# First two FFN steps in halves, free banks for six chunks' products, a new order of the work

## The chip, the cores and the metric

The kernel runs on one core of one Trainium2 chip. The metric is the device time of one execution, in microseconds: the median over runs, of which three were made of the kernel before.

## What is computed

A linear attention with decay, and a feed-forward block (FFN) on its output. Cut to what matters:

```python
for t in range(S):                      # attention, B=4, H=8, S=768, D=48
    cur = u * kt outer vt
    y[t] = rt @ (state + cur)
    state = w * state + kt outer vt     # w per head and channel, constant over t
x = y.transpose(0, 2, 1, 3).reshape(3072, 384)
h = x @ w_in                            # 384 -> 2048
sp = maximum(h, 0) + log1p(exp(-abs(h)))
out = (h * erf(sp)) @ w_out             # 2048 -> 384
```

## The kernel before, in words

**Attention.** The sequence is cut into pieces of 128 tokens. With four batches this makes 24 chunks of 128 tokens; chunk g is piece g // 4 of batch g % 4. For a chunk, VectorE or GpSimd scale k and r by powers of the decay (L220, L224), TensorE forms the 128x128 products A of eight heads (L307) in two PSUM banks, and VectorE copies their upper triangle (`copy_predicated`, L313 for chunks 0 to 7, L319 and L322 after that) over a tile `am` that holds the diagonal (made by ScalarE at L288 or by VectorE or GpSimd at L290). Then TensorE forms the chunk's output y from `am` and, from chunk 4 on, from the carried state `sbd` (L339), and the state's increment ds (L358). The diagonal's factors come from L270, L273, L277, and for the first four chunks from L233 and small products (L239, L248). y is split into a high part (ScalarE, L379) and the remainder (VectorE, L382) of the tile x: four chunks fill one x tile of 512 tokens.

**FFN.** The matrices are multiplied in fp32r, which keeps fewer bits, so every operand is split into a high and a low part and three products are summed. A step n of the FFN is one block of 512 tokens times one of 16 slices of 128 hidden columns: there are 96 steps. `f1` (L398 to L407) makes h with 9 matmuls of 128x512; ScalarE and VectorE make the activation (L412 to L437: a, b, z, c, d, e, g), its high part gh (L443, ScalarE) and low part gl (L448, VectorE or GpSimd); `f2` (L453 to L465) adds 9 matmuls to three accumulator banks. The weights arrive as 64-bit floats, are turned to fp32 by bit operations (L125 to L135) and split (L137), 16 pieces in all. Blocks 0 and 1 are done in two halves of the hidden columns, with their partial sums stored to DRAM and loaded again.

**What sets the order.** Every engine runs its instructions in the order in which the program issues them, and that order is written out by hand in one long string, `ORDER` (L694 to L757). Each word is one step: a letter for the operation, a number for the chunk or FFN step, then `+` for GpSimd, `*` for ScalarE, nothing for the default engine, and after `@` the PSUM banks. The words that this document speaks of:

- L load of a chunk (SyncE's queue), F load of a weight piece, C its conversion, W some dummy matmuls;
- K and R scaling of k and r (L220, L224), E their product (L233), B, J, H, Qc the small products that give the first chunks' diagonal (L239, L245, L248, L253), Qa, Qb, Qc for later chunks the same by L270, L273, L277, M the diagonal tile (L288, L290), N a scaled k (L228, or ScalarE's copy L266), V transposes (L259);
- A, P, Y, D: products A (L307), triangle copies P (L313), output y (L339), state increment ds (L358); S the state's update (L370, L372, L376);
- Xa, Xb: x high (L379) and x low (L382);
- f, a, b, z, c, d, e, g, h, l, p: FFN step (f L405, z L421, g L437, h L443, l L448, p L464);
- O the outputs and partial sums, Z the check at the end (L510 to L514).

PSUM has eight banks: three with the tag `h` (the h of FFN steps and others), two `A0`, `A1`, three accumulators `acc0` to `acc2`. A step whose bank or input isn't ready waits, and everything behind it on its engine with it.

**The end.** After the last step the kernel counts decay values outside a range (L510 to L513), every engine loads the count to a register (`values_load`, L514, which shows as `TENSOR_LOAD`), and a branch (L596) runs a second, general version of the whole computation if the count isn't zero. It is zero here, so that version is jumped over.

```python
    with tc.If(rv > 0, preferred_fallthrough_block=False), ...
```

Of the kernel before, what the change touches and what calls it, by code (L numbers as in the profile page):

```python
# [697 lines left out]
Q4a+ Q4b V2 L5a W3 M20* L3b C10b Q4c T0 D3@0 C10c P20 Y2 M40+ M41* C10d L5b Q5a C10e C10f+ K5+ N4 F01 R5+ Q5b Q5c X1b
A4@h1 N2* S3a* S3b* Y3@h X2a D2@0 X3a X2b S2b* X3b f0 C01a P41 S2a C01b P40 L6a C01c R6 M51* L6b Q6a+ M50* a0 K6 C01d
b0 F02 z0 Y4@h X4a A5 P51 C01e C01f+ f1 D4 c0 P50 d0 Q6b+ X4b S4b S4a e0 g0 L7a C02a C02b Q6c C02c a1 b1 Y5 X5a X5b z1  # L700
f2 M60* c1 C02d C02e K7 M61+ A6 d1 N5 f3 P61 D5 P60 C02f+ S5b h0 a2 N6+ e1 S5a g1 F11 L7b C11a b2 C11b h1 l0 Y6 z2 a3
b3 D6 X6a S6b S6a c2 d2 l1+ e2 f4 C11c p0 p1 a4 Q7a C11d z3 C11e g2 h2 C11f Q7b+ Q7c f5 l2+ c3 X6b F03 C03a C03b C03c
# [124 lines left out]
```

## Time and profile before

| | |
|---|---|
| median of 3 runs (510.79, 512.91, 512.54) | 512.54 us |
| profiled execution, its own time | 510.69 us |
| span of that execution, first to last instruction | 508.9 us |
| TensorE busy | 493.1 us, 97% |
| ScalarE busy | 403.3 us, 79% |
| VectorE busy | 338.1 us, 66% |
| GpSimd busy | 183.1 us, 36% |
| DMA, mean rate over the span | 93 GB/s |
| granted TensorE clock, mean | 0.996 |

The profiled execution was 1.85 us shorter than the median. Busy shares are averages over the whole span: the page's second part cuts it into 40 slices, and the first three slices and the last one differ from the rest.

### The profile page before, as it was taken

To read this page: it belongs to the slowest core of one execution; us is meant where nothing else is said; L and a number is where in the kernel's file an instruction comes from. 1 tells how busy PE (TensorE), PEld (TensorE's weight loads), DVE (VectorE), ACT (ScalarE), POOL (GpSimd) and SP (SyncE) were. 2 spreads that over 40 slices of the span, in tenths; PEclk is the share of its full clock that TensorE was granted. 3 is DMA by queue.
4 is the path that set the end of the run, shared out by engine and by line. 5 is a ranking of instruction groups with operands and counts; after the bars stand their busy time and mean duration, and the time that the engine had idled before them with its cause. 6 is when DMAs were issued, how large, how long until landed. Compare 5 with 4: busy or idle time off the path is not lost.

```text
span 508.9 us, 10505 instructions
## 1 busy us (share of the span) xinstructions
PE 493.1 (97%) x4176; PEld 389.5 (77%) x4176; DVE 338.1 (66%) x610; ACT 403.3 (79%) x747; POOL 183.1 (36%) x167
## 2 busy tenths in 40 slices
PE   7789999999999999999999999999999999999994
PEld 3567777877877777787878888787888888878883
DVE  7999999898876956765868644646556453353442
ACT  4788999999997666778776777878778777987982
POOL 6657335433265544625354033513312221202110
PEclk9999999999999999999999999999999999999998
DMA  8656343613605151250131350020120000000001
GB/s 309 222 215 247 123 154 125 216 62 116 243 23 182 64 166 50 90 190 13 51 134 43 105 190 0 7 87 1 63 91 0 1 2 0 33 31 1 0 1 68
DMA packets 14007, 47.34 MB, mean 93 GB/s; under 512 B 1664, under 2 KB 2560, under 8 KB 13952
## 3 DMA queue, kind: packets, MB, share of 16 engines
q1 hardware_dynamic: 13952, 46.61, 26.7%
q8 instruction: 35, 0.57, 0.5%
q14 instruction: 20, 0.16, 0.1%
HBM read 40.31 MB, written 6.29 MB: 92 GB/s over the span
## 4 chain that ended last, share of the span: by engine, by line
PE 86%; DVE 8%; ACT 2%; DMA 1%; issue 1%; POOL 1%; DVEq 0%; ACTq 0%; POOLq 0%
PE h L405 38%; PE acc L464 36%; PE y L339 6%; PE A L307 3%; PE ds L358 1%; DVE s L421 1%; DVE am L313 1%; DMA out_dram<-o 1%; DVE att L220 1%; DMA o<-part 1%; DVE wt L129 1%; DVE gl L448 1%; ACT gh L443 0%; DVE att L224 0%; DVE s L437 0%
## 5 line engine op out<-in xcount | busy, mean ns | idle before, releaser
L405 PE MATMUL h<-x,wih 128*128 128x512 f32 x576 | 183.1, 399 | 1.4 <-DVE s L437 1.0
L448 POOL TENSOR_TENSOR gl<-s,gh 128x512 fp32r<-128x512 f32 x52 | 69.0, 1328 | 213.9 <-ACT gh L443 186.6
L405 PEld LDWEIGHTS h<-x,wih 128*128 128x128 f32 x576 | 106.7, 188 | 28.3 <-DVE s L437 1.9
L464 PE MATMUL acc<-gh,woh 128*128 128x512 f32 x288 | 115.0, 399 | 0.0
L464 PE MATMUL acc<-gl,woh 128*128 128x512 f32 x288 | 114.1, 396 | 0.2 <-DVE gl L448 0.2
L405 PE MATMUL h<-x,wil 128*128 128x512 f32 x288 | 113.7, 395 | 0.0
L464 PE MATMUL acc<-gh,wol 128*128 128x512 f32 x288 | 113.7, 395 | 0.0
L437 DVE SCALAR_TENSOR_TENSOR s<-s,h 128x512 f32<-128x512 f32 x96 | 65.6, 685 | 61.4 <-ACT s L433 61.1
L421 DVE SCALAR_TENSOR_TENSOR s<-s,h 128x512 f32<-128x512 f32 x96 | 65.7, 686 | 59.3 <-ACT s L416 42.4
L425 ACT ACTIVATE s<-s 128x512 f32<-128x512 f32 x96 | 60.2, 628 | 37.3 <-DVE s L421 37.3
L443 ACT CAST gh<-s 128x512 fp32r<-128x512 f32 x96 | 58.7, 614 | 21.6 <-DVE s L437 16.0
L412 ACT ACTIVATE s<-h 128x512 f32<-128x512 f32 x96 | 56.7, 592 | 15.6 <-PE h L405 15.1
L464 PEld LDWEIGHTS acc<-gl,woh 128*128 128x128 f32 x288 | 54.2, 188 | 14.0 <-DVE gl L448 1.5
L464 PEld LDWEIGHTS acc<-gh,woh 128*128 128x128 f32 x288 | 54.1, 188 | 13.4 <-ACT gh L443 0.2
L405 PEld LDWEIGHTS h<-x,wil 128*128 128x128 f32 x288 | 54.1, 188 | 12.9
L464 PEld LDWEIGHTS acc<-gh,wol 128*128 128x128 f32 x288 | 54.2, 188 | 12.7
L416 ACT ACTIVATE s<-s 128x512 f32<-128x512 f32 x96 | 60.4, 632 | 2.1
L433 ACT ACTIVATE s<-s 128x512 f32<-128x512 f32 x96 | 60.3, 629 | 2.1
L429 ACT ACTIVATE s<-s 128x512 f32<-128x512 f32 x96 | 60.4, 629 | 1.9
L448 DVE TENSOR_TENSOR gl<-s,gh 128x512 fp32r<-128x512 f32 x44 | 31.6, 719 | 13.7 <-ACT gh L443 13.1
L290 POOL TENSOR_TENSOR am<-ident,q 128x512 f32<-128x512 f32 x17 | 19.0, 1118 | 25.9 <-DVE q L277 17.6
L339 PE MATMUL y<-am,att 128*32 128x128 f32 x768 | 25.5, 273 | 1.5 <-DVE am L313 1.3
(98 smaller groups left out, 514.0 us busy)
## 6 DMA issues: line engine op xcount, KB each, us to landing
att<-in_att_dram SPq DMA_DIRECT2D x24, 512.0 KB, 4.0
att<-in_att_dram SPq DMA_DIRECT2D x20, 608.0 KB, 5.6
raw<-in_win_dram SPq DMA_DIRECT2D x8, 768.0 KB, 6.4
raw<-in_wout_dram SPq DMA_DIRECT2D x8, 768.0 KB, 4.7
out_dram<-o SPq DMA_DIRECT2D x17, 256.0 KB, 2.2
part<-o SPq DMA_DIRECT2D x6, 256.0 KB, 3.8
o<-part SPq DMA_DIRECT2D x6, 256.0 KB, 4.2
att<-in_early_dram SPq DMA_DIRECT2D x4, 224.0 KB, 8.2
```

The source lines that it names most:

```text
L339: nc.tensor.matmul(out=y[r:r + 32, q, :], lhsT=lhsT, rhs=rhs, start=r not in new, stop=True, skip_group_check=True)
L405: nc.tensor.matmul(out=h, lhsT=w[:, f, q, :], rhs=x[:, xi, q, :], start=k == 0, stop=k == 8)
L412: nc.scalar.activation(out=s1, in_=e["h"], func=AF.Tanh, bias=FB0, scale=FA0)
L416: nc.scalar.activation(out=s1, in_=s1, func=AF.Tanh, bias=FB1, scale=FA1)
L421: nc.vector.scalar_tensor_tensor(out=e["s"], in0=e["s1"], scalar=FG, in1=e["h"], op0=ALU.mult, op1=ALU.add)
L425: nc.scalar.activation(out=s, in_=s, func=AF.Tanh, bias=FB2, scale=FA2)
L429: nc.scalar.activation(out=s, in_=s, func=AF.Square, bias=FB3, scale=FA3)
L433: nc.scalar.activation(out=s, in_=s, func=AF.Square, bias=FB4, scale=FA4)
L437: nc.vector.scalar_tensor_tensor(out=s, in0=s, scalar=FC, in1=ff[n]["h"], op0=ALU.subtract, op1=ALU.mult, reverse0=True)
L443: nc.scalar.copy(out=e["gh"], in_=e["s"])
L448: eng.tensor_tensor(out=e["gl"], in0=e["s"], in1=e["gh"].bitcast(F32), op=ALU.subtract)
L464: nc.tensor.matmul(out=acc[e], lhsT=w[:, f, es], rhs=g, start=first and i == 0, stop=last and i == 2)
```

## The change

- `f1` can make a step in two calls: `f0x` and `f1x` multiply only the first 256 tokens of block 0 (chunks 0 and 1) into the left half of the bank, and the later words `f0`, `f1` the other 256 (chunks 2 and 3) into the right half.
- The names of two more banks (`acc0`, `acc1`) are added to the table, and `turn_k` takes its bank from the word; A, Y, D and V of the first chunks then name banks that are free at that time.
- `ORDER` is another string, with the same set of steps but for the two halves. Some steps change engine: over the whole program VectorE does K for three chunks more, N for five and R for two fewer, and the low part l for five FFN steps more; GpSimd the reverse; ScalarE makes 13 diagonal tiles where it made 16.
- The last block's outputs: each of the last two accumulators is copied half by VectorE and half by ScalarE, and stored by one DMA (before: one by VectorE, one by ScalarE in two halves with two DMAs).
- The check's word Z0 stands a few steps before the end and no longer loads the register; the `values_load` stands after the last step, and the branch is given without its option.

```diff
-    def turn_k(g):
-        tp = bank("h" if g < 4 else "A1", [P, NPAIR, PR], f"kt{g}")
+    def turn_k(g, tag):
+        tp = bank(tag, [P, NPAIR, PR], f"kt{g}")
...
-    def f1(n):
+    def f1(n, half=False):
         b, f = order[n]
         x = xts[b]
-        h = ps3.tile([P, TB], F32, tag="h", name=f"h{n}")
+        cols = slice(0, TB)
+        if half:
+            cols = slice(0, TB // 2)
+        elif n in ff:
+            cols = slice(TB // 2, TB)
+        if n not in ff:
+            ff[n] = dict(h=ps3.tile([P, TB], F32, tag="h", name=f"h{n}"))
         k = 0
         for q in range(NQ):
             for w, xi in ((wih, 0), (wih, 1), (wil, 0)):
-                nc.tensor.matmul(out=h, lhsT=w[:, f, q, :], rhs=x[:, xi, q, :], start=k == 0, stop=k == 8)
+                nc.tensor.matmul(out=ff[n]["h"][:, cols], lhsT=w[:, f, q, :], rhs=x[:, xi, q, cols],
+                                 start=k == 0, stop=k == 8)
                 k += 1
-        ff[n] = dict(h=h)
...
-            if n == NS - 1 and e == 2:
-                o = outs[n, e] = tuple(fp.tile([P, TB // 2], F32, tag="s1", name=f"o{n}_{e}{i}") for i in range(2))
-                for i in range(2):
-                    nc.scalar.copy(out=o[i], in_=acc[e][:, i * TB // 2:(i + 1) * TB // 2])
-                return
-            o = outs[n, e] = fp.tile([P, TB], F32, tag="o", name=f"o{n}_{e}")
+            o = outs[n, e] = fp.tile([P, TB], F32, tag="s1" if n == NS - 1 and e == 2 else "o", name=f"o{n}_{e}")
...
-            elif n == NS - 1 and e == 1:
-                nc.vector.tensor_copy(out=o, in_=acc[e])
+            elif b == NB - 1 and e > 0:
+
+                nc.vector.tensor_copy(out=o[:, 0:TB // 2], in_=acc[e][:, 0:TB // 2])
+                nc.scalar.copy(out=o[:, TB // 2:TB], in_=acc[e][:, TB // 2:TB])
...
-        return nc.values_load(fi, min_val=0, max_val=PR)
...
+    rv = nc.values_load(fi, min_val=0, max_val=PR)
     xp2_pool.close()
-    with tc.If(rv > 0, preferred_fallthrough_block=False), tc.tile_pool(name="gen", bufs=1) as gen:
+    with tc.If(rv > 0), tc.tile_pool(name="gen", bufs=1) as gen:
...
-BANKS = {"0": "A0", "1": "A1", "h": "h", "2": "acc2"}
+BANKS = {"0": "A0", "1": "A1", "h": "h", "2": "acc2", "3": "acc0", "4": "acc1"}
...
-L0a K0 V0 L3a K3 W2 L1a R0 E0 K1 W3 R3 B0@1 J0* E3+ H0 Q0c* R1 A0 M00* P00 B3@2 J3* F00 H3 V1 E1 L2a L0b L2b M01+ B1@h
+L0a K0 W2 W3 L1a R0 E0 W2 R1 L3a R3 B0@0 J0* H0 Q0c* K3 M01 K1 M00* V0@1 A0@34 P01 F00 P00 E3 E1+ V1@h N0* L0b D0@1 B1
...
```

The order on TensorE before its first FFN steps. The names: y3 is the output of chunk 3, ds3 its state increment, h0 and h1 the banks of FFN steps 0 and 1, x0 the tile of block 0, A4 the products of chunk 4; "..." stands for rows that repeat. Before:

```order
L339 MATMUL y3_567<-am3_1_385,att3_188 32x128
L339 MATMUL y3_567<-am3_0_394,att3_188 32x128 x2
L339 MATMUL y3_567<-am3_1_385,att3_188 32x128 x5
L358 MATMUL ds2_585<-att2_254 48x48 x8
L405 MATMUL h0_598<-x0_404,wih_89 128x512 x2
L405 MATMUL h0_598<-x0_404,wil_90 128x512
...
L339 MATMUL y4_639<-att4_423,sbd_160 32x128 x12
L339 MATMUL y4_639<-am4_0_524,att4_423 32x128 x2
```

With the change:

```order
L307 MATMUL A4_1_576<-att4_425 64x128
L411 MATMUL h0_603<-x0_357,wih_89 128x256 x2
L411 MATMUL h0_603<-x0_357,wil_90 128x256
...
L411 MATMUL h1_620<-x0_357,wih_89 128x256 x2
L411 MATMUL h1_620<-x0_357,wil_90 128x256
...
L411 MATMUL h0_603<-x0_357,wih_89 128x256 x2
L411 MATMUL h0_603<-x0_357,wil_90 128x256
...
L339 MATMUL y4_650<-att4_425,sbd_160 32x128 x12
L339 MATMUL y4_650<-am4_0_556,att4_425 32x128 x2
```

Step 0 came after y of chunk 2 and ds of chunk 3, whole, and step 1 only after y of chunk 4 and the products A of chunk 5. Now the left halves of both steps stand directly behind the products A of chunk 4, and the right half of step 0 behind them. The same chunk products as before (Y0 to Y3, D0 to D3, A0 to A4) stand ahead of the first FFN matmul.

The order on VectorE up to the last remainder of x for block 0 (x0 from y0 to y3 are the four chunks' parts; am4, A4 belong to chunk 4, att5 to chunk 5, wt10 is a weight piece). Before:

```order
L313 COPY_PREDICATED am2_0_467<-mask_98,A2_0_426 128x512
L132 SCALAR_TENSOR_TENSOR wt10_448<-raw10_390,wt10_448 128x768
L270 TENSOR_TENSOR att5_461<-att5_461,ub_85 128x384
L228 TENSOR_TENSOR att4_423<-att4_423,wkn_159 128x384
L273 TENSOR_TENSOR att5_461<-att5_461 128x384
L277 TENSOR_REDUCE q5_542<-att5_461 128x8
L382 TENSOR_TENSOR x0_404<-y1_365,x0_404 128x3x128
L382 TENSOR_TENSOR x0_404<-y2_507,x0_404 128x3x128
L382 TENSOR_TENSOR x0_404<-y3_567,x0_404 128x3x128
L313 COPY_PREDICATED am4_1_526<-mask_98,A4_1_546 128x512
```

With the change:

```order
L313 COPY_PREDICATED am2_1_418<-mask_98,A2_1_479 128x512
L313 COPY_PREDICATED am2_0_517<-mask_98,A2_0_478 128x512
L382 TENSOR_TENSOR x0_357<-y1_390,x0_357 128x3x128
L132 SCALAR_TENSOR_TENSOR wt10_436<-raw10_423,wt10_436 128x768
L270 TENSOR_TENSOR att5_461<-att5_461,ub_85 128x384
L273 TENSOR_TENSOR att5_461<-att5_461 128x384
L277 TENSOR_REDUCE q5_570<-att5_461 128x8
L382 TENSOR_TENSOR x0_357<-y3_499,x0_357 128x3x128
L313 COPY_PREDICATED am4_1_558<-mask_98,A4_1_576 128x512
L220 TENSOR_TENSOR att5_461<-att5_461,wk_117 112x512
L382 TENSOR_TENSOR x0_357<-y2_536,x0_357 128x3x128
L313 COPY_PREDICATED am4_0_556<-mask_98,A4_0_575 128x512
```

The last three parts of x stood together, so both halves of block 0 became ready at once. Now chunk 1's part comes first, with a weight conversion, the diagonal of chunk 5, a triangle copy of chunk 4 and a scaling of chunk 5 between it and the last part, chunk 2's.

The end of TensorE's queue (acc0 to acc2 are the last accumulators, cnt the check's count). Before:

```order
L464 MATMUL acc80_2_5031<-gl_95_5453,woh_91 128x512
L464 MATMUL acc80_2_5031<-gh_95_5442,wol_92 128x512
L512 MATMUL cnt_5478<-bad_5476,mask_98 1x4
L514 TENSOR_LOAD fi_179
L596 COMPARE_AND_BRANCH
L596 UNCONDITIONAL_BRANCH
```

With the change:

```order
L470 MATMUL acc80_2_5045<-gh_95_5462,woh_91 128x512
L470 MATMUL acc80_2_5045<-gl_95_5464,woh_91 128x512
L470 MATMUL acc80_2_5045<-gh_95_5462,wol_92 128x512
L594 TENSOR_LOAD fi_179
L596 COMPARE_AND_BRANCH
```

The check's matmul is gone from behind the last accumulation, and one branch follows the register load where two did.

## Rows read from the trace of the kernel before

**Rows 1.** The page's first part: busy us of an engine, share of the span, instructions.

```profile
PE 493.1 (97%) x4176; PEld 389.5 (77%) x4176; DVE 338.1 (66%) x610; ACT 403.3 (79%) x747; POOL 183.1 (36%) x167
```

**Rows 2.** Stretches of time: length, busy us of PE, PEld, DVE, ACT, POOL; clock, DMA share, GB/s.

```profile
30.00:40.00 10.00, 9.64 (x196) 7.38 (x189) 9.96 (x18) 8.74 (x22) 6.60 (x4) 1.00 0.53 194
80.00:90.00 10.00, 10.00 (x72) 7.87 (x72) 9.71 (x14) 9.87 (x18) 4.38 (x3) 1.00 0.30 108
120.00:130.00 10.00, 10.00 (x106) 8.01 (x105) 8.52 (x14) 9.78 (x18) 1.30 (x1) 1.00 0.64 210
480.00:509.00 29.00, 22.48 (x97) 17.30 (x95) 10.29 (x17) 18.06 (x33) 2.59 (x2) 0.92 0.09 30
```

**Rows 3.** TensorE's timeline before the stream: start us, us, work, idle before with its releaser.

```profile
22.40 0.33 PE L248 MATMUL qp<-ident,att 128*128 128x128 f32 x1 [1.49 <-DVE att L245]
29.23 1.08 PE L339 MATMUL y<-am,att 128*32 128x128 f32 x32 [1.34 <-DVE am L313]
```

**Rows 4.** The chain that ended last, 33 to 41 us: start us, us, what.

```profile
33.70 2.13 PE h L405 x8
35.83 1.67 PE y L339 x56
37.50 1.03 PE A L307 x32
38.53 2.29 PE h L405 x9
```

**Rows 5.** VectorE's timeline, 10 to 34 us: columns as in rows 3.

```profile
10.68 1.28 DVE L224 TENSOR_TENSOR att<-att,wre 112x512 f32<-112x512 f32 x2
13.10 0.73 DVE L313 COPY_PREDICATED am<-mask,A 128x512 f32<-128x512 uint32 x1 [1.13 <-POOL att L233]
16.14 0.69 DVE L290 TENSOR_TENSOR am<-ident,q 128x512 f32<-128x512 f32 x1
19.45 2.08 DVE L132 SCALAR_TENSOR_TENSOR wt<-raw,wt 128x768 int32<-128x768 int32 x1
22.38 0.36 DVE L370 COPY sbd<-ds 48x192 f32<-48x192 f32 x1
29.07 1.18 DVE L132 SCALAR_TENSOR_TENSOR wt<-raw,wt 128x768 int32<-128x768 int32 x1
30.18 0.55 DVE L270 TENSOR_TENSOR att<-att,ub 128x384 f32<-128x384 f32 x1
32.16 1.49 DVE L382 TENSOR_TENSOR x<-y,x 128x384 fp32r<-128x384 f32 x3
```

**Rows 6.** ScalarE's and GpSimd's timelines, one row each, same columns.

```profile
11.73 1.28 ACT L288 ACTIVATE am<-ident,q 128x128 f32<-128x128 f32 x4
...
19.68 1.04 POOL L290 TENSOR_TENSOR am<-ident,q 128x512 f32<-128x512 f32 x1
```

**Rows 7.** TensorE's timeline: four transposes, each with its own weights.

```profile
25.11 0.55 PE L259 MATMUL kt<-ident,att 112*128 112x112 f32 x4
```

**Rows 8.** TensorE's timeline inside the stream: where it stood idle.

```profile
67.82 0.86 PE L339 MATMUL y<-att,sbd 112*32 112x128 f32 x24 [0.34 <-DVE am L313]
...
181.40 0.73 PE L405 MATMUL h<-x,wih 128*128 128x512 f32 x2 [1.00 <-DVE s L437]
```

**Rows 9.** The page's groups: busy us, mean ns of one, idle before.

```profile
L437 DVE SCALAR_TENSOR_TENSOR s<-s,h 128x512 f32<-128x512 f32 x96 | 65.6, 685 | 61.4 <-ACT s L433 61.1
```

**Rows 10.** End of the program: timeline, then lines L514, L596, L822 (count, ns min/median/max, first and last start).

```profile
502.12 0.40 PE L464 MATMUL acc<-gh,wol 128*128 128x512 f32 x1
...
L514 PEldq TENSOR_LOAD <-fi x1: 774/774/774, 503.2 to 503.2; - x1
...
L596 PEldq COMPARE_BRANCH  x2: 95/1892/3690, 504.1 to 504.4; - x2
...
L822 DVEq DRAIN  x2: 10/34/57, 507.3 to 508.5; - x2
L822 PEldq DRAIN  x2: 8/40/73, 508.1 to 508.5; - x2
```

More of the change, by code (lines that the diff above doesn't have):

```diff
@@ L470, in put_out @@
         o = outT[b] if blk is None else outT[bass.ds(blk, 1)].rearrange("a p n -> (a p) n")
-        o = o[e * P:(e + 1) * P]
-        if isinstance(outs[n, e], tuple):
-            for i in range(2):
-                nc.sync.dma_start(out=o[:, i * TB // 2:(i + 1) * TB // 2], in_=outs[n, e][i])
-        else:
-            nc.sync.dma_start(out=o, in_=outs[n, e])
+        nc.sync.dma_start(out=o[e * P:(e + 1) * P], in_=outs[n, e])
     outs = {}
@@ L529, in body @@
             f2(num, "xyz".index(sub))
+        elif what == "f" and sub == "x":
+            f1(num, True)
         elif what in steps:
@@ L542, in body @@
         elif what == "V":
-            turn_k(num)
+            turn_k(num, BANKS[where or "h"])
         elif what == "Z":
-            rv = count_bad()
+            count_bad()
         elif what == "Q":
@@ L698 @@
[L698 to L702, printed above, removed]
@@ new lines @@
+f10 b9 R9+ h7 l7 z9 p7 c8 d8 e8 g8 Q9c C05c K9+ C05d c9 d9 O70a a10 O70b e9 A9 h8 O72a l8+ g9 M90+ b10 f11 z10 h9 C05e
+C05f+ c10 a11 Q8b O71a P90 d10 b11 f12 p8 l9 p9 M91 z11 a12 e10 F14 C14a g10 C14b C14c c11 C14d d11 e11 g11 h10 l10+
+F04 b12 C14e z12 C14f Q8c f13 R8 f14 h11 O72b l11 c12 a13 b13 d12 z13 C04a p10 C04b e12 a14 c13 d13 p11 g12 h12 b14
+f15 C04c C04d S5c+ C04e C04f e13 l12+ a15 p12 M81 g13 O71b z14 F15 C15a C15b b15 F06 h13 l13 c14 S5d z15 f16 p13 d14
+e14 c15 g14 d15 e15 h14 l14+ C15c C15d C15e g15 a16 b16 f17 h15 S6c+ P91 p14 C15f z16 l15 C06a a17 b17 C06b C06c z17
@@ new lines @@
+O232a D9 S9b L11a d24 e24 Y8 D8@h S8b S8a K11+ L11b R11+ Q10c a25 b25 z25 c25 d25 e25 p22 p23 S9a g24 h24 O231b g25
+S9d+ L12a X8a f26 l24 S8d+ f27 f28 O232b X8b R10 O231c a26 a27 b27 O230a O230b O230c h25 l25 b26 M101+ O232c A10 z26
+c26 z27 c27 d26 e26 d27 Q11a p24 p25 g26 e27 g27 h26 l26+ a28 f29 h27 l27+ b28 P101 z28 M100* Q11b+ N11+ Q11c a29
+M111+ b29 z29 c28 d28 e28 S7d+ P100 S7c c29 d29 M110+ p26 N10+ p27 e29 A11 Y10@h g28 h28 D10@h g29 f30 X10a P110 h29
+X10b a30 P111 f31 S10a L13a l28+ Y11 R13+ b30 S10b a31 D11 K13 z30 c30 p28 L12b d30 e30 Q12a+ L14a b31 Q12b+ X11a l29
@@ new lines @@
+c38 a39 N14 b39 z39 d38 c39 O312c p36 p37 e38 X13b S12b S12d d39 e39 g38 h38 K16 g39 f40 h39 R15+ M140* Q15a+ Q15b+
+f41 f42 M141+ X12a X12b a41 l39+ b41 l38 Q15c a40 S10c+ b40 z40 c40 d40 p38 p39 z41 e40 g40 c41 d41 e41 g41 a42 h40
+S11c+ f43 h41 M150+ l40 a43 b43 A14 l41 P141 b42 S10d z43 c43 d43 z42 L16b Q16a p40 p41 K15+ A15@h1 R16+ c42 M151+
+P140 d42 e42 P151 Q16b+ g42 h42 l42+ e43 g43 N15+ h43 l43+ Y14 D14 X14a X14b P150 Q16c S14b f44 f45 L18a a44 b44 S14d+
+z44 S14a a45 Y15 X15a X15b b45 z45 D15 L18b S15a p42 f46 c44 S15b L17a L17b K18+ M161+ d44 K17+ e44 g44 h44 Q18a M160
@@ new lines @@
+g60 h60 p59 l60+ X19a z61 f62 a62 b62 c61 d61 e61 z62 X19b c62 p60 d62 e62 S19a g61 M210+ h61 g62 f63 Q22b+ a63 b63
+l61 z63 h62 l62 f64 f65 c63 d63 e63 p61 a65 b65 g63 h63 A21 P210 a64 S17c+ b64 z64 M200+ c64 l63+ d64 e64 S18c+ z65
+p62 p63 O630a O630b M211 P211 g64 h64 c65 d65 e65 g65 A20 Y21@h P200 X21a O631a X21b O632a h65 f66 f67 L23a a66 b66
+a67 b67 f68 l65 l64+ p64 z66 a68 c66 d66 p65 M201+ e66 P201 g66 h66 z67 R23+ c67 d67 l66 f69 b68 e67 z68 c68 S16c+
+Q22c p66 g67 R22+ A22 Y20@h O632b d68 e68 a69 M221 h67 l67+ g68 L23b Q23a f70 h68 l68+ b69 z69 c69 p67 d69 e69 g69
@@ new lines @@
+X20a Q23b+ Q23c M230* p68 a70 h69 b70 z70 c70 d70 e70 X20b P221 l69 f71 f72 a71 b71 g70 z71 h70 p69 c71 l70+ d71 e71
+g71 h71 l71 a72 b72 f73 a73 f74 z72 b73 z73 p70 p71 c72 d72 e72 g72 h72 K23+ A23@h1 c73 S19c+ l72+ d73 e73 g73 a74 b74
+z74 p72 h73 l73+ c74 d74 e74 f75 g74 h74 M220 a75 b75 l74 M231 P230 z75 c75 d75 e75 p73 p74 g75 f76 f77 P231 a76 b76
+h75 l75+ Y23@1 P220 Y22 z76 c76 d76 e76 g76 a77 f78 h76 l76 b77 z77 c77 d77 e77 f79 a79 g77 X22a X22b X23a X23b a78
+p75 p76 N22 h77 b78 z78 O631b b79 l77+ c78 d78 e78 z79 g78 h78 p77 l78+ c79 d79 e79 g79 f80 a80 b80 z80 h79 f81 c80
@@ L758 @@
+h91 l91+ b93 z93 e92 g92 h92 c93 f94 d93 f95 a94 b94 e93 l92 p91 p92 a95 b95 z94 c94 g93 Z0 h93 l93 d94 p93x p93y z95
+e94 g94 c95 h94 p93z l94 d95 e95 p94x p94y g95 h95 l95 p94z p95x O950a O950b p95y O951a O951b p95z O952a O952b
 """
```

93 lines of the change are left out of this document (35 added, 58 removed).

## The prediction

> **What bounds the kernel now.** Start with the page's busy shares: TensorE is busy 97% of the span, no other engine over 79% [rows 1]. That is an average, so the next view is the table of stretches [rows 2]. From 30 us on TensorE is all but full (9.64 of 10 us, then 10.00), and the last 29 us hold 22.48 busy us. So three places can give time: the start, before TensorE has FFN work; the short waits inside the stream; and the end, after its last matmul.
>
> The start is VectorE's: between 30 and 40 us it is busy 9.96 of 10 us [rows 2], and TensorE's two longest waits before the stream, 1.49 and 1.34 us, both end on a VectorE copy [rows 3]. The chain of waits then shows FFN step 0 from 33.70 us, right behind three low parts of x that end at 32.16 + 1.49 = 33.65 [rows 4, 5]. From there TensorE goes on without a gap: step 0, y, A, step 1 [rows 4]. Whoever brings the last x part earlier moves everything behind it, provided the other engines follow.
>
> Inside the stream two waits stand out, 0.34 and 1.00 us [rows 8]. At the end the last matmul is over at 502.12 + 0.40 = 502.52, yet the span ends at 508.9. TensorE's load of the check's register starts only at 503.2, and of its two branches one takes 3.69 us from 504.4 on; its drain at 508.1 is the last of the engines', VectorE's is at 507.3 [rows 10].
>
> **The change, part by part.**
>
> *Start, work on VectorE.* I count words up to a point in both orders. Up to the remainder of chunk 1, which the left halves need, the new queue has gained M01, K2 and a Qa: 0.69 + 0.64 + 0.55 = 1.88 us, K at half of the pair's 1.28 us [rows 5]. Gone or put behind it are one weight piece's last operation (1.18), four operations of the 0.55 us kind, two low parts (1.49 / 3 = 0.50 each) and three small copies at 0.36 at most: 1.18 + 2.20 + 1.00 + 1.08 = 5.46 us [rows 5]. E3 and E1 change places for nothing. So the point comes 3.6 us earlier.
>
> Up to the remainder of chunk 2, which the right halves need, the queue has gained M01, K2, K5, a Qa and a triangle copy, 0.69 + 2 x 0.64 + 0.55 + 0.73 = 3.25 us, against one 0.55 and three 0.36, 1.63 us: 1.6 us more work [rows 5].
>
> *Start, a wait that goes.* VectorE stood for 1.13 us before its first triangle copy [rows 5]. The row names GpSimd, but ScalarE's diagonal tile, begun at 11.73 and taking 1.28 us [rows 6], ends at 13.01, just before that copy at 13.10. In the new order the first tile copied is made by VectorE itself (M01), and the first E stands one step further ahead, so that ScalarE's tile is there when its copy comes. I take the 1.13 us as gone; bounds 0 and 1.13.
>
> Together: the left halves can start at 33.65 - 3.6 - 1.1 = about 29 us, the right ones at 33.65 + 1.6 - 1.1 = 34.1.
>
> *Start, the halves on TensorE.* No 256-column matmul is in the trace. From below, half of a step's 2.29 us [rows 4] is 1.15 us; from above a half costs a whole step, 2.29, if loading weights set the pace. The nearest row with short matmuls and own weights is the transposes, 0.55 / 4 = 0.14 us each with 112 columns [rows 7], 1.24 us for nine. I take 1.2. Both left halves, 2.4 us, then run from 29 to about 31.5, inside time in which TensorE would wait for VectorE: they cost nothing. If that cover were gone they would cost 2.4 us. What is left: half of step 0, y, A, half of step 1, that is 34.1 + 1.2 + 1.67 + 1.03 + 1.2 = 39.2 us, where before step 1 ended at 38.53 + 2.29 = 40.8 [rows 4]. D4 moves from behind step 1 to ahead of it, which for what follows is nothing. This is a gain of 1.6 us.
>
> Will the others follow? Up to the low part of step 0 VectorE's words cost within 0.3 us of the same in both orders, so it comes out ahead by the 1.13 us. I take 1.5 us for the start, between 1.1 and 1.6; with the bounds of the halves (right halves at 2.29 each) and of the wait, -0.1 to 2.0.
>
> *Collisions on VectorE.* The weight operation that took 2.08 us at 19.45, against 1.18 at 29.07, ran while GpSimd made a diagonal tile from 19.68 for 1.04 us [rows 5, 6]. The change moves K2, K5 and M01 from GpSimd to VectorE and puts E2 where the tile was. One collision for another: 0, bounds 0.9 us each way, the difference of the two rows.
>
> The Trainium skill, "SBUF — State Buffer", section "Who interferes with whom", has a rule for this: a VectorE instruction with two SBUF inputs and a GpSimd instruction that reads SBUF exclude each other, whoever comes second waiting in full. The two rows agree with it: one waited, in 0.9 us more. The rule speaks against the change, since the moved K and M instructions have two SBUF inputs themselves: beside E1, E2 and the next tile that would be two such waits more than now, and the sum would be 2.8 - 2 x 0.9 = 1.0 us in place of 2.8.
>
> *Banks and loads.* A0, A1, V1 and others take free banks; their waits don't show as rows of over 0.4 us, so nothing is gained but what the order uses. In SyncE's queue chunk 3's V load moves ahead of chunk 1's and chunk 1's first load ahead of chunk 3's; all these are issued long before use, and none of the waits named above ends on a DMA: 0.
>
> *Inside the stream.* 0.34 and 1.00 us of waits [rows 8] may go or come elsewhere; a new order has its own. I take 0.4 us off, between 1.3 off and 1 more.
>
> *End.* Without the check's matmul behind it, TensorE's register load (0.77 us) can begin at 502.5 instead of 503.2, and one branch follows, not two, 504.1 to 504.4 [rows 10]: 0.7 + 0.3 = 1.0 us. The block that is jumped over still lies between the branch and the end, so I keep the 3.69 us. VectorE's drain at 507.3 is the next, and it moves up by some 0.3 us for the same reason, so the end can't come more than 508.1 - 507.0 = 1.1 earlier. I take 0.9; bounds 0.3 and 1.1. The halved copies lie on ScalarE and VectorE behind the last matmul, hidden by that jump; without the jump they would be on the path.
>
> **Sum.** 1.5 + 0 + 0.4 + 0.9 = 2.8 us. The profiled execution, 510.7 us with a span of 508.9, would become 507.9 with a span of 506.1. It was 1.85 us under the median of the runs shown, so against the median, 512.54, this is 509.7 us. A measurement of this kernel can tell about 0.5%, 2.6 us, from no change: the forecast lies on that line.
>
> **Rivals.**
>
> *More than that.* Both stream waits go (1.3), the start gives 2.0 and a collision of 0.9 goes as well: 2.0 + 0.9 + 1.3 + 1.0 = 5.2 us, 507.3 us. For it: VectorE is full at the start, so each wait taken from it counts. Against: all must fall together. Chance 0.17.
>
> *Only the end counts.* From 80 to 90 us ScalarE is busy 9.87 and VectorE 9.71 of 10 us [rows 2], beside a full TensorE. If they, not TensorE, set the pace between 60 and 140 us, the start's 1.5 us is a longer wait later, and 0.9 to 1.2 us remain: about 511.5 us. Against: VectorE's and ScalarE's sums up to steps 0 to 6 hardly change, and they too start earlier. Chance 0.13.
>
> *Two collisions more.* If each of GpSimd's E1, E2 and its next tile holds up a VectorE operation once, by the 0.9 us between 2.08 and 1.18 [rows 5], where now one does, 2 x 0.9 = 1.8 us go and with them the start's gain: 2.8 - 1.8 = 1.0 us faster, 511.5 us. Against: three operations have left GpSimd's queue there, so it runs less beside VectorE. Chance 0.07. (It is the case of the skill's rule above.)
>
> *The halves do nothing.* The left halves also need the low weights that GpSimd makes, and the new ORDER gives GpSimd E1 and E2 before them; if these came after 34 us, the halves would wait with the rest, 2.8 - 1.5 = 1.3 us faster, 511.2. Against: GpSimd has less to do before them than now. Counted with the two cases above, 0.20 together.
>
> *Slower: steps 17 to 24 starve.* Up to VectorE's first operation of step 19 the new order puts 25 instructions and takes 20 away; at the rows' durations (0.69 us for FFN operations [rows 9], 0.55 to 1.18 for the others [rows 5]) that is about 5.6 us more work ahead of it. VectorE has 1.5 us free in 10 there, ScalarE 0.2 [rows 2]. If the free time can't be used, TensorE stands up to 5.6 us between 115 and 150 us: 509.7 + 5.6 = 515.3 us. It decides against the change from 2.8 us of new idle on. For it: TensorE is never idle there now, so any lag shows. Against: the same order also puts one more FFN step of TensorE (2.29 us a product [rows 4]) ahead, and the free time of 30 us is 4.5 us. Chance 0.08.
>
> **How the numbers follow.** The forecast has 0.55, spread evenly about 2.8 us between 1.6 and 4.0: 0.30 of it lies beyond 2.6 us, 0.25 within. Faster by over 0.5%: 0.30 + 0.17 = 0.47. Within: 0.25 + 0.20 = 0.45. Slower: 0.08. The range leaves out the slower case and the far end of the first rival: from 507.0 to 513.0 us, with the spread of the runs shown, 2 us, in it.
>
> **What would show it.** In the changed profile: matmuls of 128x256 near 29 us, followed by a wait of TensorE of up to 3 us that ends on a low part of x (still L382) near 34 us; half steps of 1.2 us; step 1 complete near 39 us; no wait of over 1 us before VectorE's first triangle copy; TensorE's idle between 40 and 500 us at most 1.5 us; its register load near 502.5 less the shift, one branch of some 3.7 us, and some 5.4 us from the last matmul to the end of the span where it was 6.4. The prediction is wrong if the left halves don't run before 31 us, if idle of over 2 us appears between 60 and 160 us, or if the long branch is gone or doubled.

## The result

The changed kernel took 514.41 us (median of 8 runs, 513.53 to 517.04), the kernel before 511.59 us beside it (8 runs, 510.61 to 512.91): ratio 1.0054, 95% interval 1.0036 to 1.0073. It is slower by about 2.8 us, where 2.8 us faster was forecast, and lies outside the range.

The profiled execution of the changed kernel has a span of 512.2 us (508.9 before). TensorE's timeline, which answers to [rows 3, 8] and to the end of [rows 10] (start us, us, work, idle before with its releaser):

```profile
22.96 0.33 PE L248 MATMUL qp<-ident,att 128*128 128x128 f32 x1 [2.82 <-DVE att L245]
23.59 1.86 PE L339 MATMUL y<-am,att 128*32 128x128 f32 x32 [0.30 <-DVE am L313]
...
33.57 0.51 PE L411 MATMUL h<-x,wih 128*128 128x256 f32 x2
...
35.70 0.28 PE L411 MATMUL h<-x,wil 128*128 128x256 f32 x1
...
50.73 0.86 PE L339 MATMUL y<-att,sbd 112*32 112x128 f32 x24 [0.82 <-DVE am L313]
...
53.02 0.56 PE L358 MATMUL ds<-att 128*48 128x48 f32 x16 [0.55 <-DVE att L228]
...
100.64 0.73 PE L411 MATMUL h<-x,wih 128*128 128x512 f32 x2 [0.45 <-DVE s L443]
...
493.45 0.39 PE L470 MATMUL acc<-gh,woh 128*128 128x512 f32 x1
...
506.15 0.40 PE L470 MATMUL acc<-gh,wol 128*128 128x512 f32 x1
```

The last matmul ends at 506.15 + 0.40 = 506.55, 4.03 us later than before; from there to the end of the span it is 512.2 - 506.55 = 5.65 us, where it was 6.4. So the new end gives back some 0.7 us, and the stream has lost 4. The left halves begin at 33.57, not at 29; ahead of them stands a wait of 2.82 us. Behind that wait a product of 1.08 us [rows 3] takes 1.86. The table of stretches says why (columns as in [rows 2]):

```profile
20.00:30.00 10.00, 6.88 (x132) 4.63 (x128) 8.68 (x12) 5.37 (x18) 3.83 (x4) 0.83 0.46 163
24.00:27.00 3.00, 3.00 (x35) 1.50 (x29) 3.00 (x7) 2.19 (x7) 0.00 (x0) 0.50 0.21 26
```

From 24 to 27 us TensorE's granted clock is 0.50: 1.2 GHz, where 1.00 is 2.4. What TensorE waited for was a small copy on VectorE. VectorE's timeline and then GpSimd's, to be set beside [rows 5, 6]:

```profile
11.62 0.69 DVE L290 TENSOR_TENSOR am<-ident,q 128x512 f32<-128x512 f32 x1
12.89 1.36 DVE L313 COPY_PREDICATED am<-mask,A 128x512 f32<-128x512 uint32 x2
...
19.25 3.45 DVE L290 TENSOR_TENSOR am<-ident,q 128x512 f32<-128x512 f32 x1
22.62 0.28 DVE L245 COPY att<-qp 128x128 f32<-128x128 f32 x1
...
47.72 1.95 DVE L132 SCALAR_TENSOR_TENSOR wt<-raw,wt 128x768 int32<-128x768 int32 x1
...
84.61 1.83 DVE L454 TENSOR_TENSOR gl<-s,gh 128x512 fp32r<-128x512 f32 x1 [0.90 <-ACT gh L449]
```

```profile
17.46 1.94 POOL L233 TENSOR_TENSOR att<-att 112x512 f32<-112x512 f32 x1 [3.17 <-DVE att L220]
19.35 1.05 POOL L290 TENSOR_TENSOR am<-ident,q 128x512 f32<-128x512 f32 x1
20.35 1.80 POOL L137 TENSOR_TENSOR wil<-wt,wih 128x768 fp32r<-128x768 f32 x1
...
47.56 1.29 POOL L220 TENSOR_TENSOR att<-att,wk 112x512 f32<-112x512 f32 x1
...
84.61 1.29 POOL L224 TENSOR_TENSOR att<-att,wr 112x512 f32<-112x512 f32 x1
85.86 1.75 POOL L220 TENSOR_TENSOR att<-att,wk 112x512 f32<-112x512 f32 x1
```

At 11.62 VectorE makes a diagonal tile (L290) in 0.69 us. At 19.25 it makes another of the same size, chunk 1's first (word M10), in 3.45 us. Its end, 22.70, is 0.55 us behind the end of GpSimd's third instruction, 20.35 + 1.80 = 22.15. GpSimd ran E2, the tile M30 and the weight remainder C00f without a gap, and VectorE's instruction stood through the rest of the first and all of the other two, 2.76 us more than it takes alone; such a stay is called a lockout below. A second, smaller case stands at 47.72: 1.95 us for a weight operation that takes 0.95 to 0.96 alone, to the end of the one GpSimd instruction that ran when it came (47.56 + 1.29 = 48.85) and 0.8 us more.

A wait through several instructions isn't the rule. At 84.61 a low part l (0.67 us alone) and a GpSimd instruction begin together, and GpSimd's next one follows without a gap. The low part ends at 84.61 + 1.83 = 86.44, 0.54 us behind the end of the first, and it is the second GpSimd instruction that pays: 1.75 us, where the same one took 1.29 at 47.56. Here VectorE was let in between.

The other loss is near the end. VectorE's and ScalarE's timelines:

```profile
495.03 0.16 DVE L508 TENSOR_TENSOR bad<-wp,wu 112x4 f32<-112x4 f32 x1
497.96 0.15 DVE L511 TENSOR_REDUCE fi<-cnt 1x1 int32<-1x4 f32 x1 [2.78 <-PE cnt L510]
```

```profile
499.47 0.63 ACT L431 ACTIVATE s<-s 128x512 f32<-128x512 f32 x1 [1.77 <-DVE s L427]
```

VectorE compares for the check (L508), and its next instruction, the reduction of TensorE's count (L511), waits 2.78 us for it. The count stood in TensorE's queue behind two whole products (p91, p92). Everything of VectorE's last steps stood behind the reduction, and ScalarE then waited 1.77 us for it. What that costs TensorE is read from the start of p91 to the last matmul's end, the same 45 matmuls in both kernels: 506.55 - 493.45 = 13.1 us, where it was 502.52 - 491.31 = 11.2, by [rows 10] and this row of the kernel before:

```profile
491.31 0.39 PE L464 MATMUL acc<-gh,woh 128*128 128x512 f32 x1
```

The instructions of the branch's line, to be set beside L596 in [rows 10]:

```profile
L596 SPq EVENT_SEMAPHORE  x8: 17/17/17, 508.5 to 510.8; - x8
L596 PEldq COMPARE_BRANCH  x1: 3658/3658/3658, 505.0 to 505.0; - x1
L596 DVEq COMPARE_BRANCH  x1: 72/72/72, 507.4 to 507.4; - x1
...
L596 DVEq EVENT_SEMAPHORE  x1: 21/21/21, 510.9 to 510.9; - x1
```

TensorE's one branch takes 3.66 us, but it begins at 505.0, ahead of the last matmul's end. VectorE's next instruction after its own branch (507.4) comes at 510.9, and SyncE's last event, the landing of the last DMA, at 510.8: these two end the program now.

### The profile page after: what moved, and what is told of

The parts are those of the page before. It is cut to its first block, busy times and chain, and to the rows that moved or that the text cites. A ratio compares the mean times of both kernels' runs of the same rounds, so it can differ in the third digit from the quotient of the medians.

```text
span 512.2 us, 10509 instructions
## 1 busy us (share of the span) xinstructions
PE 495.9 (97%) x4194; PEld 390.6 (76%) x4194; DVE 341.8 (67%) x604; ACT 402.0 (78%) x739; POOL 180.7 (35%) x173
## 4 chain that ended last, share of the span: by engine, by line
PE 65%; DVE 14%; ACT 13%; issue 4%; POOL 2%; DMA 1%; DVEq 0%; ACTq 0%; POOLq 0%
PE h L411 27%; PE acc L470 27%; PE y L339 5%; PE A L307 3%; DVE s L427 2%; ACT gh L449 2%; ACT s L431 2%; PE dummy L94 2%; DVE s L443 2%; ACT s L435 2%; ACT s L439 2%; DVE gl L454 1%; DVE am L313 1%; ACT s L418 1%; ACT s L422 1%
## 5 line engine op out<-in xcount | busy, mean ns | idle before, releaser
L411 PE MATMUL h<-x,wih 128*128 128x512 f32 (+1 forms) x588 | 183.8, 394 | 0.9 <-DVE s L443 0.5
L454 POOL TENSOR_TENSOR gl<-s,gh 128x512 fp32r<-128x512 f32 x47 | 62.6, 1334 | 217.5 <-ACT gh L449 202.2
L411 PEld LDWEIGHTS h<-x,wih 128*128 128x128 f32 x588 | 108.2, 188 | 28.1 <-DVE s L443 1.7
L411 PE MATMUL h<-x,wil 128*128 128x512 f32 (+1 forms) x294 | 114.8, 391 | 0.0
L411 PEld LDWEIGHTS h<-x,wil 128*128 128x128 f32 x294 | 55.3, 188 | 12.8 <-POOL wil L137 0.3
L454 DVE TENSOR_TENSOR gl<-s,gh 128x512 fp32r<-128x512 f32 x49 | 38.4, 787 | 11.9 <-ACT gh L449 11.6
L307 PEld LDWEIGHTS A<-att 48*64 48x64 f32 x768 | 18.9, 133 | 7.1 <-issue 5.5
```

The costliest lines, as they stand in the source:

```text
L411: nc.tensor.matmul(out=ff[n]["h"][:, cols], lhsT=w[:, f, q, :], rhs=x[:, xi, q, cols], start=k == 0, stop=k == 8)
L454: eng.tensor_tensor(out=e["gl"], in0=e["s"], in1=e["gh"].bitcast(F32), op=ALU.subtract)
```

## The experiments

All ratios are to the kernel before, timed beside each set of runs (512.26, 511.82 and 511.80 us); the changed kernel's is 1.0054 (1.0036 to 1.0073). Each run has 6 to 10 executions. Two kernels whose intervals overlap aren't told apart by the times alone.

| run | what | median us | ratio (95%) |
|---|---|---|---|
| e1_m10 | changed, M10 on ScalarE | 510.03 | 0.9945 (0.9926 to 0.9965) |
| e2_warm | changed, dummies in the wait | 512.91 | 1.0013 (0.9991 to 1.0035) |
| e3_z | changed, check in two words | 513.58 | 1.0041 (1.0012 to 1.0070) |
| e4_whole | changed, no halves | 515.90 | 1.0076 (1.0051 to 1.0100) |
| e5_end | before, with the change's end | 513.70 | 1.0044 (1.0022 to 1.0066) |
| e6_end2 | before, another end | 514.67 | 1.0063 (1.0035 to 1.0091) |
| e7_all | e1, with the end of e6 | 509.90 | 0.9960 (0.9943 to 0.9976) |
| e8_m10_whole | e1, no halves | 510.97 | 0.9978 (0.9963 to 0.9994) |
| e9_best | e1, a third end | 509.10 | 0.9931 (0.9908 to 0.9953) |
| e10_end3 | before, the end of e9 | 511.85 | 0.9986 (0.9966 to 1.0007) |
| e11_k7 | e9, K7 moved | 509.77 | 0.9946 (0.9925 to 0.9967) |
| e12_m30 | changed, M30 on ScalarE | 512.52 | 1.0023 (0.9999 to 1.0046) |

### Is it the one tile?

```diff
-... P11 X0a X0b M10
+... P11 X0a X0b M10*
```

> Only edit: chunk 1's first diagonal tile (word M10) goes from VectorE to ScalarE. Theory A (VectorE's 3.45 us at 19.25, where the same operation takes 0.69 us at 11.62, is 2.76 us of waiting behind three GpSimd instructions, and it starves TensorE for 2.82 us and drops its clock): no VectorE row over 1.5 us before 30 us, TensorE's wait at 22.96 under 1 us, granted clock 1.00 throughout 20 to 30 us, left halves at 31 us or before where they began at 33.57, and 2 to 4 us faster than the changed kernel, about 511 us. Theory B (VectorE and ScalarE set the pace until 60 us and take the gain back): left halves earlier as well, but less than 1 us faster at the end, 513.5 us or more.

TensorE's timeline and the stretch from 20 to 30 us of this run:

```profile
20.44 0.33 PE L248 MATMUL qp<-ident,att 128*128 128x128 f32 x1 [0.49 <-DVE att L245]
...
29.65 0.51 PE L411 MATMUL h<-x,wih 128*128 128x256 f32 x2
...
32.64 0.39 PE L411 MATMUL h<-x,wih 128*128 128x256 f32 x1 [0.44 <-DVE x L382]
...
38.04 0.28 PE L411 MATMUL h<-x,wil 128*128 128x256 f32 x1
```

```profile
20.00:30.00 10.00, 8.96 (x234) 7.00 (x236) 9.84 (x18) 9.57 (x32) 4.90 (x5) 1.00 0.69 244
```

The wait is 0.49 us in place of 2.82, the clock stays at 1.00, the left halves begin at 29.65, 3.9 us earlier, and the kernel is faster than the changed one by 4.4 us (medians) to 5.6 (ratios): more than theory A's 2 to 4. One word of the order decides the sign. (It also takes the tile's own 0.69 us from VectorE and gives ScalarE a tile more, 1.28 us by [rows 6]; the next run leaves the tile on VectorE.)

To see what the tile waited for, one of the three GpSimd instructions was taken away and the tile left where it was:

```diff
-... B2@2 J2 H2 M30+ P10 P30 ...
+... B2@2 J2 H2 M30* P10 P30 ...
```

> The changed kernel with chunk 3's first diagonal tile (word M30) on ScalarE in place of GpSimd; chunk 1's tile (M10) stays on VectorE. It asks what a waiting VectorE instruction waits for: Theory A (it isn't let in between GpSimd instructions that follow each other without a gap): with one of the three gone, the tile's 3.45 us become 2.3 to 2.6, the end of the weight remainder C00f plus its own 0.55 us, and the kernel is about 1 us faster, 513.3 us. Theory A2 (it waits for the one instruction that runs when it comes): 0.7 to 0.9 us, TensorE's wait of 2.82 us gone, 3 us or more faster, 511.5 us or less. Theory B (the 3.45 us are no lockout, but something of this operation): unchanged at 3.4 us, 514.4 us.

VectorE's and GpSimd's rows:

```profile
19.05 2.45 DVE L290 TENSOR_TENSOR am<-ident,q 128x512 f32<-128x512 f32 x1
```

```profile
17.25 1.94 POOL L233 TENSOR_TENSOR att<-att 112x512 f32<-112x512 f32 x1 [3.17 <-DVE att L220]
19.14 1.81 POOL L137 TENSOR_TENSOR wil<-wt,wih 128x768 fp32r<-128x768 f32 x1
```

The tile takes 2.45 us, to 21.50: C00f's end, 19.14 + 1.81 = 20.95, plus 0.55. It came while E2 ran (to 19.19) and was not let in before C00f. Theory A has 2.3 to 2.6; A2 and B fall. The kernel is 0.3% faster than the changed one, 1.6 us by the ratios, 1.9 by the medians; the intervals overlap, so it is the row that decides. What isn't shown is why VectorE was kept out here and let in at 84.61.

### What the clock cost

```diff
-... B2@2 J2 H2 M30+ ...
+... B2@2 W12@3 J2 H2 M30+ ...
```

> Only edit: 12 dummy matmuls (2.6 us at full clock, into a free bank) between TensorE's words B2 and H2, inside its 2.82 us wait; the wait itself stays. Theory A (the low clock from 23.7 to 27.1 us costs a path that ends the start): granted clock 1.00 from 23 to 28 us, the y product of 1.86 us back at 1.08, left halves 1.3 to 1.7 us earlier, at 32 us, total 1 to 1.7 us faster than the changed kernel, about 513.1 us. Theory B (VectorE is the path there, and TensorE only waits for it later): clock at 1.00 too, halves less than 0.5 us earlier, total within 0.5 us of the changed kernel, 514.4 us.

```profile
20.00:30.00 10.00, 9.40 (x187) 6.03 (x180) 10.00 (x15) 6.82 (x23) 4.66 (x4) 1.00 0.53 192
```

Dummies are matmuls whose result nobody reads. With them in the wait the clock is 1.00 through it, and the kernel 0.4% faster, 1.5 us by the medians and 2.1 by the ratios. Theory A: of what M10 cost, 1.5 to 2 us were the clock that the wait brought down. VectorE's own waiting, the rest, is still there.

### What the halves are worth

Both runs leave out the words `f0x` and `f1x`, e4 from the changed kernel, e8 from e1.

> Only edit: words f0x and f1x left out, so that FFN steps 0 and 1 are whole steps where their right halves stood. Theory A (the halves fill time in which TensorE waits, and bring it 2.2 us ahead): TensorE idle before step 0 for 2 us or more, step 2 ends up to 2.2 us later than 44.35, total 1 to 2.2 us slower than the changed kernel, 515.4 to 516.6 us. Theory B (VectorE and ScalarE set the pace until 60 us, and the waits at 50.73 and 53.02 us take up what the halves gave): total within 0.5 us of the changed kernel, 514.4 us.

> The kernel of e1_m10 without the words f0x and f1x, so that steps 0 and 1 are whole. Theory A (the halves are worth what they fill, 2.3 us less what later waits take): 1.5 to 2.3 us slower than e1_m10, 511.5 to 512.3 us, with a TensorE wait of over 1.5 us before step 0. Theory B (the halves' worth in e4_whole came from the clock that dropped a second time; without the lockout they give nothing): within 0.5 us of e1_m10, 510 us.

TensorE's row and a stretch of e4, then of e8:

```profile
38.47 0.50 PE L411 MATMUL h<-x,wih 128*128 128x512 f32 x1 [1.67 <-DVE x L382]
```

```profile
20.00:30.00 10.00, 6.85 (x91) 4.70 (x96) 8.54 (x12) 4.88 (x17) 3.28 (x4) 0.61 0.46 163
```

```profile
32.67 0.50 PE L411 MATMUL h<-x,wih 128*128 128x512 f32 x1 [1.67 <-DVE x L382]
```

```profile
30.00:40.00 10.00, 7.83 (x115) 5.90 (x116) 8.39 (x14) 8.15 (x20) 5.11 (x3) 0.83 0.49 192
```

Without halves step 0 waits 1.67 us for chunk 2's low part, and in e8 the clock falls at that wait (0.83 from 30 to 40 us, where e1 has 1.00). In e4 it was down for longer even ahead of it (0.61 from 20 to 30 us, where the changed kernel has 0.83), and this execution, 517.7 us, was among the two slowest of ten, so its price isn't that of the halves alone. Against the halves' kernels that is 1.1 us (e4, by ratios; 1.5 by medians) and 1.7 us (e8; 0.9). That is theory A at its lower edge or short of it (1 to 2.2 us in e4, 1.5 to 2.3 in e8): the halves gain about 0.9 to 1.7 us. The intervals overlap in both pairs, so the size is rough. That a part of it comes from keeping TensorE busy is argued from the clock, not shown by itself.

### The end

e5 puts the change's end alone on the kernel before.

> The kernel before with the change's end alone: the check's word at the same place between g93 and h93, the register load after the last step, the branch without its option, the last two accumulators copied half by VectorE and half by ScalarE, one DMA each. Theory A (the check's reduction stands in VectorE's queue until TensorE has done two products, which costs the stream 1 to 1.5 us; the end behind the last matmul gives back 0.7): 0.2 to 0.9 us slower than the kernel before, VectorE's wait before the reduction over 2 us, last matmul to end of span 5.7 us where it was 6.4. Theory B (the end is the gain of 0.9 us that was forecast): 0.7 to 1.1 us faster than the kernel before.

```profile
497.76 0.15 DVE L511 TENSOR_REDUCE fi<-cnt 1x1 int32<-1x4 f32 x1 [2.62 <-PE cnt L510]
```

The wait is there (2.62 us), and this end makes the kernel before slower, by 0.2 to 0.7%: theory A, and more than its 0.9 us at most. By the profile p91 to the last matmul takes 12.8 us (11.2 before), and 5.4 us follow (6.4), a net loss of 0.6; in this execution the clock was also down at the start (0.85 from 30 to 40 us, 1.00 in [rows 2]). Why the timings show 1.9 us or 0.4% rather than 0.6 isn't settled.

In e3 the comparison and the count stand earlier, behind h91, the reduction where it stood:

```diff
-h91 l91+ ... c94 g93 Z0 h93
+h91 Z0a l91+ ... c94 g93 Z0b h93
```

> Only edit: the check's word is in two: the comparison and TensorE's count of it nine words earlier on VectorE and TensorE, the reduction of the count where the word stood. Theory A (VectorE waited 2.78 us at 497.96 for a count that stood in TensorE's queue behind two whole products; the last three FFN steps came late by it): VectorE's wait before the reduction under 0.2 us, TensorE's idle after 495 us under 0.5 us where it was about 1 us, last matmul 1.2 to 1.9 us earlier, total 1.2 to 1.9 us faster than the changed kernel, about 512.9 us. Theory B (the last steps are bound by ScalarE's chain whatever VectorE does): last matmul less than 0.4 us earlier, about 514.2 us.

```profile
495.36 0.14 DVE L509 TENSOR_REDUCE fi<-cnt 1x1 int32<-1x4 f32 x1
```

```profile
503.46 0.51 PE L470 MATMUL acc<-gl,woh 128*128 128x512 f32 x1 [0.23 <-DVE gl L454]
```

The reduction waits for nothing, of TensorE's waits after 495 us the one of 0.23 is left, and p91 to the last matmul takes 11.5 us in place of 13.1, 1.6 us less. The last matmul is only 0.95 us earlier (505.59), since this execution had come to p91 0.64 us later, and the medians give 0.8 us. Theory A's wait is gone as it said, but its 1.2 to 1.9 us aren't reached; theory B (under 0.4 us) falls too. The intervals of e3 and the changed kernel overlap.

In e6, the kernel before with another end, ScalarE alone copies the last accumulators, the last one in two halves with a DMA each, and the check's words stand so close that it made the same mistake the other way round (the words of the check alone):

```diff
-g91 h91 f93 ...
+g91 h91 Z0a f93 ...
```

> The kernel before with another end: check in two (comparison and count behind g91, reduction behind g93), register load after the last step, default branch, all three last accumulators copied by ScalarE, the last in two halves with a DMA each as before. Theory A (what ends the span is TensorE's branch of 3.7 us before, and in the changed kernel the landing of the last DMA and VectorE's stay behind its branch, both 4.3 us behind the last matmul because both engines still copied): VectorE's branch is behind it early, the last half lands 2.9 us behind the last matmul, and the span ends about 4.3 us behind it where it was 6.4; no VectorE wait at the reduction; 1.7 to 2.2 us faster than the kernel before, 510 us. Theory B (some other engine's branch takes its 3.7 us after the last copy in any order): 5.5 us or more from the last matmul to the end, less than 1 us faster.

```profile
484.95 0.19 PE L521 MATMUL cnt<-bad,mask 112*1 112x4 f32 x2 [1.69 <-DVE bad L519]
```

```profile
L607 SPq EVENT_SEMAPHORE  x8: 17/17/17, 510.1 to 510.6; - x8
...
L607 SPq COMPARE_BRANCH  x1: 45/45/45, 506.8 to 506.8; - x1
```

Now TensorE's count waited 1.69 us for VectorE's comparison, with step 93 behind it. And SyncE, whose branch in the changed kernel was over in half a microsecond, stood from 506.8 to 510.1 behind it. Both theories miss: the engine that pays is another one, theory B in kind, with 7.2 us from the last matmul to the end.

> The changed kernel with chunk 1's first diagonal tile on ScalarE (as e1_m10), the check in two (as e3_z), and the end of e6_end2. Theory A (the three costs are independent): 510.0 of e1_m10, less 0.9 for the check's wait, less 1.4 for the end, 507.7 us; 4 us or more faster than the kernel before. Theory B (what is gained at the start or for the last steps is waited for at another place): 509 us or more.

e7 combines e1, the split check and that end: 509.9 us, no better than e1. Theory B: the span ends 7.0 us behind the last matmul where e1 has 5.9, as SyncE stands for 3 us behind its branch; that ate what the check's wait gave back.

e9 draws both lessons: comparison, count and reduction as three words far apart, ScalarE alone copies, one DMA for each output.

```diff
-... g82 ... p88 ... g91 ... g93 Z0 ...
+... g82 Z0a ... Z0m p88 ... g91 Z0b ... g93 ...
-                nc.vector.tensor_copy(out=o[:, 0:TB // 2], in_=acc[e][:, 0:TB // 2])
-                nc.scalar.copy(out=o[:, TB // 2:TB], in_=acc[e][:, TB // 2:TB])
+                nc.scalar.copy(out=o, in_=acc[e])
```

> The kernel of e1_m10 with another end: the check in three words, far apart (comparison behind g82, TensorE's count ahead of p88, reduction behind g91), and all three last accumulators copied whole by ScalarE, one DMA each. Theory A (each wait of the end was a wait of one queue for another, and with words far enough apart none is left): from 480 us to the last matmul TensorE stands under 0.4 us, 1.0 to 1.8 us earlier than e1_m10; VectorE's branch is over before the last copy is, the last DMA lands 3.7 to 4.0 us behind the last matmul, the span ends 5.0 to 5.3 us behind it where it was 5.9: 1.5 to 2.4 us faster than e1_m10, 508 us, and 0.7% or more faster than the kernel before. Theory B (as in e7_all, SyncE's own branch takes 3 us after the last issue, or a new wait comes): 509.5 us or more.

```profile
L596 SPq EVENT_SEMAPHORE  x8: 17/17/17, 503.9 to 506.2; - x8
...
L596 DVEq EVENT_SEMAPHORE  x1: 21/21/21, 502.9 to 502.9; - x1
...
L596 SPq COMPARE_BRANCH  x1: 45/45/45, 503.4 to 503.4; - x1
```

VectorE's branch is over at 502.9, SyncE's takes half a microsecond, and the landing of the last DMA (506.2) ends the program, 4.1 us behind the last matmul; the span ends at 507.6. The median of 509.1 us, ratio 0.9931, is the lowest of all and ahead of both kernels, though only 0.9 us ahead of e1 where 1.5 to 2.4 were expected, with intervals that overlap. So what this end is worth isn't shown by the time.

> The kernel before with the end of e9_best alone (check in three words, register load last, default branch, ScalarE's copies, one DMA each). Theory A: the stream as in the kernel before, and 5.0 to 5.3 us from the last matmul to the end of the span in place of 6.4: 1.1 to 1.4 us faster than the kernel before. Theory B (SyncE's branch takes 3 us here): 6.5 us or more behind the last matmul, no faster than the kernel before.

e10, that end on the kernel before, is inconclusive: the interval of the ratio reaches from a gain of 1.7 us to none. Its profile shows 5.3 us behind the last matmul, as theory A has it, in an execution whose mean clock was 0.991.

### The second lockout

```diff
-... P60 K7+ P61 b2 g1 C02f+ X5b ...
+... P60 P61 b2 g1 C02f+ K7+ X5b ...
```

> e9_best with one word moved: K7, GpSimd's scaling of chunk 7, behind C02f in GpSimd's order, so that it doesn't follow M61 directly. Theory A (the VectorE weight operation of 1.95 us at 47.72 in the changed kernel waited 1.0 us for K7, and TensorE's waits of 0.82 and 0.55 us at 50.73 and 53.02 come from it): that operation under 1.1 us, the first of the two waits gone, 0.5 to 1.0 us faster than e9_best. Theory B (the next wait takes it up, or K7 collides with another VectorE operation later): within 0.4 us of e9_best.

VectorE's, GpSimd's and TensorE's rows:

```profile
44.28 0.96 DVE L132 SCALAR_TENSOR_TENSOR wt<-raw,wt 128x768 int32<-128x768 int32 x1
...
48.38 3.02 DVE L454 TENSOR_TENSOR gl<-s,gh 128x512 fp32r<-128x512 f32 x1
```

```profile
47.99 1.61 POOL L220 TENSOR_TENSOR att<-att,wk 112x512 f32<-112x512 f32 x1
49.55 1.30 POOL L454 TENSOR_TENSOR gl<-s,gh 128x512 fp32r<-128x512 f32 x1
```

```profile
56.55 0.73 PE L411 MATMUL h<-x,wih 128*128 128x512 f32 x2 [0.89 <-DVE s L443]
...
62.09 1.10 PE L307 MATMUL A<-att 48*64 48x128 f32 x32 [1.07 <-issue]
```

The weight operation is back at 0.96 us and the wait of 0.82 us before y is gone, but two others of 0.89 and 1.07 us stand a little later. Theory B: nothing is gained. The moved K7 (47.99) now meets a low part on VectorE, which takes 3.02 us where it takes 0.67 alone: it stands through K7 and through the GpSimd instruction behind it, to 49.55 + 1.30 = 50.85 and 0.55 us more. ScalarE then waits 2.36 us, and TensorE's 0.89 us end on a later operation of the same two engines. The wait of 1.07 us has no releaser in the profile; its cause stays open.

## Why the prediction was wrong

*Start, work on VectorE, and the wait that goes: right.* The 1.13 us before the first triangle copy are gone (12.89, no wait). Without M10's long stay the left halves begin at 29.65 and the right ones go on from 32.64 (e1, where VectorE is also spared the tile's own 0.69 us), against a forecast of about 29 and 34.1.

*Start, the halves: the half step right, its worth too high.* Eighteen half matmuls run from 33.57 to 35.70 + 0.28 = 35.98, 1.2 us a half step (1.2 forecast). In the sum two of them, under cover, stand for 2 x (2.29 - 1.2) = 2.2 us; e4 and e8 put the halves at 0.9 to 1.7. The start as a whole is more than the 1.5 us taken: in e1 step 1 is complete at 38.04 + 0.28 = 38.32, where 39.2 was forecast and 40.8 stood before.

*Collisions: the step that failed.* It said "One collision for another: 0, bounds 0.9 us each way", the difference of two rows. The row it took as the price, 2.08 us at 19.45 [rows 5], was itself a wait through two GpSimd instructions, the one of [rows 6] (19.68 to 20.72) and the one ahead of it, which ran when it came:

```profile
18.44 1.28 POOL L233 TENSOR_TENSOR att<-att 112x512 f32<-112x512 f32 x1 [2.64 <-DVE att L224]
```

The row it was set against, 1.18 us at 29.07, wasn't undisturbed either: GpSimd made a tile from 27.75 for 1.69 us, and the same operation takes 0.95 us at 38.11. The price of one collision is not bounded by one overlap, then: it can be the rest of a train of GpSimd instructions, for M10 three, 2.76 us. What it stops was not priced either: the copy behind M10, on which TensorE waited 2.82 us, and TensorE's clock. e1 puts the whole at 4.4 to 5.6 us, where the rival of two collisions more had 1.8 us. The sentence that speaks for this failure stood in the prediction: by the rule of the Trainium skill, "SBUF — State Buffer", section "Who interferes with whom", whoever comes second waits in full. The trace agrees, and e12 adds that the wait can reach over GpSimd's next instructions too, as it did for M10, though not for the low part at 84.61.

*End: half right.* Behind the last matmul 0.7 us were gained (0.9 forecast, 0.3 to 1.1), one branch is left, and it takes 3.66 us (3.69 kept). But the step counted only what leaves TensorE's queue. It did not ask what stands behind the moved check in VectorE's: 2.78 us of waiting, and of the stream 0.95 us by e3's last matmul or 1.6 by the stretch from p91 on (e3, and the same stretch in e5). Also, the branch of TensorE is not what ends the program now: VectorE's branch and the last DMA do. VectorE had been named as the next.

*Stream: within its bounds, but the wrong way.* The two waits of [rows 8] are gone or smaller, and others stand at 50.73, 53.02 and 100.64, 1.8 us together against 1.3. Between 40 and 500 us TensorE is busy 457.1 of 460 us, 458.4 before: 2.9 us idle, where at most 1.5 was forecast; 0.4 of it belongs to the check.

*The rivals.* The slower one, steps 17 to 24, did not come: between 101 and 169 us TensorE stands nowhere for 0.1 us. The test "if the left halves don't run before 31 us" told it: they ran from 33.57. (One sum of the chances is off by a little: of 0.55 spread evenly from 1.6 to 4.0 us, 0.32 lies beyond 2.6 us, not 0.30.)

So the sum's gains were there, 2.8 us of them and more (e1: 2.2 us faster than the kernel before by the medians, 2.8 by the ratio, with the bad end still in it), and one VectorE instruction of 0.69 us outweighed them.

## What to carry to other kernels

Before a two-input VectorE instruction is moved, look at what GpSimd runs at that time: as an upper bound price it with the whole train of GpSimd instructions that follow without a gap, and then with what waits behind it. A small computation that goes from VectorE to TensorE and back is a word in each of two queues: each part must stand so far behind the other that neither queue waits. At the end of a program write down for each engine when its last own instruction lets it go; the last of these, not the longest, ends it.
